# One matmul between two inner steps, a peak one chunk earlier, a store on another queue and an earlier flag load in a hash-attention and MLP kernel

## The chip, the cores and the metric

The kernel runs on one core of a Trainium2 chip. A core has five engines with queues of their own: TensorE (PE, with weight loads as PEld), VectorE (DVE), ScalarE (ACT), GpSimd (POOL) and SyncE (SP). SP, ScalarE and GpSimd issue DMA transfers. The metric is the device time of one execution in microseconds; lower is better.

## What is computed

```python
def _attn_ref(q, k, v, proj):                      # (4, 8, 768, 64) each, proj (64, 6)
    q_bucket, k_bucket = ...                       # 6 sign bits of q @ proj and k @ proj
    mask = q_bucket[:, :, :, None] == k_bucket[:, :, None, :]
    scores = np.where(mask, scale * np.matmul(q, k.transpose(0, 1, 3, 2)), -1e9)
    attn = softmax(scores)                         # sums have 1e-9 added
    return np.matmul(attn, v)

def _moe_ref(x, w_in, w_out):                      # x (3072, 512), d_ff 2048
    h = x @ w_in
    r = np.maximum(h, 0.0)
    return (r * r) @ w_out
```

The attention's output, its heads side by side, is the x of the second block.

## The kernel before

**Stages.** The first half of the span is the attention, pair of heads by pair of heads. Its softmax takes no maximum off; that is right as long as no score is large. So the second half also finds the largest sum of squares of any piece of q and k (a *peak*, 32 pieces of 128x768), and a flag says at the end whether a slow general path (`general`, line 1906) has to run instead. With the inputs here it does not run.

The second half is the two matrix products in three chunks of 1024 tokens (`i` = 0, 1, 2). Each chunk has a *hidden* stage (x times w_in, then relu squared, into the tiles b11 to b22) and a *project* stage (times w_out).

**Products by Strassen's scheme.** Each product is done with seven block products instead of eight (`product`, line 976, whose inner names one, two, three and five are copies of accumulators to SBUF by ScalarE at line 995). In the project stage there are seven outer products, k = 0 to 6, of seven inner ones each; an inner one (`add`, line 983) is four 128x256 matmuls at line 988. The order of the adds in `product` is fixed: acc[0] (copied to `one`), acc[1], acc[0] (copied to `two`), acc[2] (to `five`), acc[0] (to `three`), acc[2], acc[0].

**The hidden stage of chunks 1 and 2** runs `hidden_wide` (line 1329), twice for each n: half 0 and half 1. Of the seven outer factors, two are done whole: two 512-wide matmuls each at line 1313 (`add` in `outer_steps`, one per f in 0, 1) into the accumulator acc0. The others are split again: `inner_steps` (line 1226) gives four steps for each. In half 0 these are A and D. A step is one or two 256-wide matmuls at line 1245 into banks of PSUM, and a copy of a bank by ScalarE (lines 1255, 1261, 1264, 1271, 1279). The next step of the same factor adds into that same bank, so it waits until the copy has read it. For n = 0, half 0 has its own order, written out at lines 1341 to 1357; ScalarE copies the finished acc0 to the tile `tmp` (`two`, line 1324), which is used at line 1377.

**Peaks.** `mark` (line 1046) puts a peak into ScalarE's queue at the place where it stands (square with a sum, line 1039), and issues on GpSimd's queue the loads of the piece that the mark after the next will use (`load_peak`, line 1029, two buffers). The marks stand in the hidden stage's steps, in `rest` (called in the hook after acc[1]), `beside` (after `three`) and, where `then` has it, right after the copy to `two`. Chunk 1 has two in each k; chunk 2 has two in k = 0 and three in each k of 1, 2 and 3.

**Stores.** `put_out` (line 1598) turns a finished output block on VectorE and stores it in four pieces of 32 rows: those of the quarter (1, 1) on GpSimd's queue, all others on SP's. The last quarter of chunk 2 goes in parts (`put_part`, `put_last`): n = 0 on SP, n = 3 and n = 1 on SP and ScalarE in turn, n = 2 in two transfers at the very end. `in_turn` keeps their order of issue. The quarters come in the order n = 0, 3, 1, 2. From n = 3 on a scheduler places the instructions (`by_hand.close()`); before that they stand in the order of the code.

**Semaphores of transfers.** Each transfer issued by SP or ScalarE signals its end on one of eight semaphores, which are given out in turn over the whole program, and waits before its issue for the transfer that had the same one before. GpSimd's transfers have another eight of their own. At the end of the program SP waits for all sixteen and some others, in a fixed order: those of GpSimd first, then the eight of SP and ScalarE from the first to the last.

**The flag.** `values_load(slow)` (line 1007) makes each engine load the flag into a register; the branch at line 1933 reads it.

Of the kernel before, what the change touches and what calls it, by code (L numbers as in the profile page):

```python
# [34 lines left out]
def kernel(  # L35
# [10 lines left out]
    nc = tc.nc  # L46
# [9 lines left out]
    NFT = DM // P  # L56
# [10 lines left out]
    NCHUNK = B * S // NCH  # L67
# [704 lines left out]
    with by_hand:  # L772
# [532 lines left out]
        def outer_steps(i, n, half):  # L1305


            w, bt = w_unit.pop(i * NR + 2 * n + half), factors_x(i)
            acc = ps_m.tile([P, 512], FP32, name="acc0")

            def add(to, a, b, first, last):
                for f in range(NFT // 2):
                    nc.tensor.matmul(  # L1313
                        out=to, lhsT=w[:, PLACE[a], f], rhs=bt[b](f),
                        start=first and f == 0, stop=last and f == NFT // 2 - 1,
                        skip_group_check=True,
                    )

            def keep(of, name):
                if (name, half) == ("two", 0):  # L1320
                    t = p_y.tile([P, HN], FP32, name="tmp")
                else:
                    t = p_r.tile([P, 512], FP32, name=name, bufs=KEPT[name])
                nc.scalar.copy(out=t, in_=of)
                return t

            return w, acc, add, keep

        def hidden_wide(i, n, half):

            r0, r = n, NQ + n
            edge = (i, n) == (NCHUNK - 1, NQ - 1)
            w, acc, add, keep = outer_steps(i, n, half)
            own = own_factors(w, half)
            if half == 0:
                load_inner(i, n + 1)
                load_third_inner(i, n + 1, nc.sync)
                A = now["A"] = inner_steps(i, 0, w_inner[i, n][0], n > 0)
                D = now["D"] = inner_steps(i, 3, lambda a: own[a], n > 0)
                if n == 0:  # L1340
                    add(acc, 0, "11", True, False)
                    one = keep(acc, "one")
                    A[0]()
                    sums_inner(i, (3,))
                    mark()
                    add(acc, 4, "t2", False, True)
                    two = keep(acc, "two")
                    A[1]()
                    D[0]()
                    mark()  # L1350
                    A[2]()
                    D[1]()
                    A[3]()
                    D[2]()
                    sums_inner(i, (4,))
                    D[3]()
                    add_to(b11[:, r0], A[4][0], one)
                else:
                    A[0]()
                    D[0]()  # L1360
                    add(acc, 0, "11", True, False)
                    behind(0)
                    one = keep(acc, "one")
                    behind(1)
                    A[1]()
                    D[1]()
                    A[2]()
                    D[2]()
                    add_to(b11[:, r0], A[4][0], one)
                    behind(2)  # L1370
                    add(acc, 4, "t2", False, True)
                    two = keep(acc, "two")
                    A[3]()
                    behind(3)
                    D[3]()
                now["two"] = two
                add_in(D[4][0], two)
                gate_in(b11[:, r0])
                behind(4)
                sum_unit(i * NR + 2 * n + 1)  # L1380
                return
            A, D, two_0 = now["A"], now["D"], now["two"]
            B, C = inner_steps(i, 2, w_inner[i, n][2]), inner_steps(i, 1, w_inner[i, n][1])
            E = inner_steps(i, 4, lambda a: own[a])
            u0 = D[4]
            add(acc, 0, "11", True, False)
            one = keep(acc, "one")
            add_to(b11[:, r], A[4][1], one)
            B[0]()
            C[0]()  # L1390
            E[0]()
            gate_in(b11[:, r])
            behind(5)
            sum_unit(i * NR + 2 * n + 2)
            add(acc, 4, "t2", False, True)
            two = keep(acc, "two")
            add_in(u0[1], two)
            B[1]()
            C[1]()
            B[2]()  # L1400
            E[1]()
            C[2]()
            B[3]()
            E[2]()
            hB, hC, hE = B[4], C[4], E[4]

            def ahead(m):
                minus(b_t[:, m], b12[:, m], b11[:, m])

            def over(m):  # L1410
                minus(b12[:, m], b22[:, m], b12[:, m])

            put(hB[0], b12[:, r0], u0[0])
            C[3]()
            E[3]()
            if edge:
                ahead(r0)
                inner_sums(0, slice(n, n + 1))
                add_to(b22[:, r0], u0[0], hE[0])

                def hook():
                    add_to(b12[:, r], hB[1], u0[1])
                    gate_in(b12[:, r])
                    add_in(two, hE[1])
                    add_to(b21[:, r], hC[1], two)
                    add_to(b22[:, r], u0[1], hE[1])

                def with_two():
                    gate_in(b22[:, r0])
                    add_in(two_0, hE[0])  # L1430
                    add_to(b21[:, r0], hC[0], two_0)

                def with_five():
                    gate_in(b22[:, r])
                    over(r0)
                    over(r)

                def with_three():
                    gate_in(b21[:, r0])
                    gate_in(b21[:, r])  # L1440

                now["edge"] = dict(
                    hook=hook, early=lambda: ahead(r), two=with_two, five=with_five, three=with_three
                )
                return
            add_to(b22[:, r0], u0[0], hE[0])
            both = slice(n, NR, NQ)

            def sums_0():
                if i == 1:  # L1450
                    add_to(b12[:, r], hB[1], u0[1])
                else:
                    put(hB[1], b12[:, r], u0[1])
                add_to(b22[:, r], u0[1], hE[1])

            def gates_0():
                gate_in(b22[:, r0])

            def sums_1():
                add_in(two_0, hE[0])  # L1460
                add_to(b21[:, r0], hC[0], two_0)
                add_in(two, hE[1])

            def sums_2():
                add_to(b21[:, r], hC[1], two)

            def gates_1():
                if i == 1:
                    gate_in(b12[:, r])

            def gates_2():
                gate_in(b22[:, r])

            def gates_3():
                gate_in(b21[:, r0])

            def gates_4():
                gate_in(b21[:, r])

            steps = (  # L1480
                (sums_0, gates_0), (sums_1,),
                (sums_2, gates_1, lambda: ahead(both), gates_2, gates_3),
                (lambda: inner_sums(0, slice(n, n + 1)),), (gates_4,), (lambda: over(both),),
            )
            for m, some in enumerate(steps):
                behind_pair[m] = list(some)
# [111 lines left out]
        def put_out(i, ih, jh, n, o):  # L1598
# [4 lines left out]
            m0 = ih * HD + n * P  # L1603
            at = slice(i * NCH + jh * HN, i * NCH + (jh + 1) * HN)
            for a in range(P // 32):
                queue = nc.gpsimd if (ih, jh) == (1, 1) else nc.sync
                queue.dma_start(
                    out=out[at, m0 + a * 32:m0 + (a + 1) * 32].rearrange("(c i) j -> i c j", i=32),
                    in_=ot[a * 32:(a + 1) * 32].rearrange("i (c j) -> i c j", j=32),
                )  # L1610
# [11 lines left out]
        def put_part(n, o):  # L1622
# [6 lines left out]
            lo = (NCHUNK - 1) * NCH + col * QN  # L1629
            m0 = HD + row * P  # L1630
            for a in range(P // 32):
                in_turn(LATE[n][a].dma_start(
                    out=out[lo:lo + QN, m0 + a * 32:m0 + (a + 1) * 32].rearrange(
                        "(c i) j -> i c j", i=32
                    ),
                    in_=ot[a * 32:(a + 1) * 32].rearrange("i (c j) -> i c j", j=32),
                ))

        def put_last(n, o):

# [25 lines left out]
        def project(i):  # L1666
# [56 lines left out]
                close(1, 0, n)  # L1723

            more = i + 1 < NCHUNK
            uses = first_, seventh, fifth, third, second, sixth, fourth
            for k in range(7):
                b = OUTER[k][1]
# [40 lines left out]
                    minus(y21, y21, t2)  # L1769

                def rest():
                    if marks(i, k):
                        mark()
                    if (i, k) == (NCHUNK - 1, 4):
                        tops()
# [28 lines left out]
                        edge["early"]()  # L1804
                        turn_inner()

                then = {"two": mark} if i == NCHUNK - 1 and 0 < k < 4 else {}
                if edge:
                    then = dict(edge, five=lambda: (edge["five"](), rest()))
                product(  # L1810
# [301 lines left out]
```

## Time and profile before

| | |
|---|---|
| time, median of 3 runs | 847.46 us (847.46 to 849.12) |
| the profiled execution's own time | 848.54 us |
| its span, first to last instruction | 847.0 us |
| granted TensorE clock | 0.999 of full speed |
| instructions | 17534 |
| hidden stage of chunk 1, half 0 of n = 0 | from 494.8 us |
| project stage of chunk 1, k = 3 | from 620.3 us |
| hidden stage of chunk 2, half 0 of n = 0 | from 668.7 us |
| project stage of chunk 2, k = 0 | from 757.0 us |
| last transpose on TensorE | 843.1 us |

The profile is one execution. Its times are microseconds from the span's start; an engine's busy time leaves out register, branch, semaphore and DMA-issuing instructions, which the views by source line show as the engine's queue (SPq, ACTq, POOLq). A 32-bit matmul is recorded as two records: x4 of a 512-wide matmul are two matmuls. Ends of matmuls are modelled, so TensorE's pace is read from start to start.

### The profile page before, as it was taken

What the parts mean: (1) busy time and instruction counts of PE and PEld (TensorE: products, weight loads), DVE (VectorE), ACT (ScalarE), POOL (GpSimd) and SP (SyncE); (2) the same over time, 40 slices, a digit from 0 to 9 for tenths busy, and PEclk for the clock granted to TensorE, in tenths of its full rate; (3) what the DMA queues carried; (4) which work ended last, traced back from release to release, by engine and by line L of the source; (5) the groups of instructions that cost most, each with busy time, mean ns of one, the idle gap of its engine ahead of it and who ended that gap; (6) DMA issues with size and microseconds to landing.
All of it is one profiled execution on the core that took longest, in us unless ns stands there. A gap on an engine that the chain in (4) does not pass through costs nothing.

```text
span 847.0 us, 17534 instructions
## 1 busy us (share of the span) xinstructions
PE 841.0 (99%) x6710; PEld 558.3 (66%) x6710; DVE 748.7 (88%) x1081; ACT 461.3 (54%) x873; POOL 169.0 (20%) x285
## 2 busy tenths in 40 slices
PE   9999999999999999999999999999999999999998
PEld 4475444444444445544788877777888877778886
DVE  4898999999999988989899988868999877889787
ACT  5787787878777762222111148866322477765411
POOL 1321111303122200653121230002212400002202
PEclk9999999999999999999999999999999999999999
DMA  9966999978987626999977995418978964317767
GB/s 184 192 136 136 188 186 199 194 181 199 258 197 229 214 70 227 338 306 308 354 250 244 264 216 166 134 56 284 310 214 242 242 220 129 128 43 225 245 175 146
DMA packets 238296, 174.23 MB, mean 206 GB/s; under 512 B 166008, under 2 KB 196288, under 8 KB 238208
## 3 DMA queue, kind: packets, MB, share of 16 engines
q1 hardware_dynamic: 199792, 93.03, 44.5%
q0 software_dynamic: 16880, 43.92, 16.4%
q10 hardware_dynamic: 21536, 36.12, 13.9%
q8 instruction: 54, 0.88, 0.5%
q14 instruction: 34, 0.28, 0.1%
HBM read 129.64 MB, written 42.73 MB: 204 GB/s over the span
## 4 chain that ended last, share of the span: by engine, by line
PE 97%; ACT 1%; DVE 1%; DMA 1%; issue 0%; ACTq 0%; POOL 0%; POOLq 0%
PE acc L988 39%; PE st L478 18%; PE xo L532 15%; PE acc L1245 10%; PE acc L1313 7%; PE last L1245 4%; PE tot L589 1%; PE hash L396 1%; DMA raw_qk<-in_k_dram 1%; PE tp L342 0%; PE last L1313 0%; PE xo L371 0%; ACT b L1293 0%; DVE b L1303 0%; ACT raw_qk L1039 0%
## 5 line engine op out<-in xcount | busy, mean ns | idle before, releaser
L484 ACT ACTIVATE e<-st 128x768 f32<-128x768 f32 x192 | 155.5, 810 | 56.4 <-PE st L478 52.1
L532 PE MATMUL xo<-e,v_nat 64*64 64x385 f32 (+1 forms) x1520 | 156.9, 483 | 0.0
L988 PE MATMUL acc<-b,leaf 128*128 128x256 f32 x600 | 133.3, 379 | 0.4 <-ACT five L995 0.4
L988 PEld LDWEIGHTS acc<-b,leaf 128*128 128x128 f32 x600 | 113.8, 190 | 16.8 <-ACT five L995 0.8
L478 PE MATMUL st<-feat 64*64 64x384 f32 x1056 | 108.1, 482 | 0.0
L444 POOL DMA_DIRECT2D bits<-signed x120 | 62.2, 521 | 206.5 <-ACT signed L433 204.7
L532 PEld LDWEIGHTS xo<-e,v_nat 64*64 64x64 f32 (+1 forms) x1520 | 58.9, 133 | 65.3 <-issue 54.5
L988 PE MATMUL acc<-t,leaf 128*128 128x256 f32 x336 | 76.0, 379 | 0.0
L988 PEld LDWEIGHTS acc<-t,leaf 128*128 128x128 f32 x336 | 63.8, 190 | 8.8 <-issue 0.2
L478 PE MATMUL st<-bits 64*64 64x384 bf16 x768 | 66.2, 324 | 0.1
L520 DVE TENSOR_TENSOR total<-total,e 128x1536 f32<-128x1536 f32 x32 | 56.0, 1749 | 7.6 <-ACT e L484 6.8
L1034 POOL DMA_DIRECT2D raw_qk<-in_q_dram x32 | 17.3, 541 | 213.3 <-ACT raw_qk L1039 111.0
L520 DVE TENSOR_TENSOR t_x<-t_x,e 128x1536 f32<-128x1536 f32 x32 | 55.8, 1744 | 3.8 <-ACT e L484 3.7
L988 PE MATMUL acc<-x,w_unit 128*128 128x512 f32 (+1 forms) x144 | 56.5, 545 | 0.0
L478 PEld LDWEIGHTS st<-feat 64*64 64x64 f32 x1056 | 38.4, 133 | 27.3 <-issue 24.2
L988 PE MATMUL acc<-b_t,leaf 128*128 128x256 f32 x240 | 53.8, 379 | 0.0
L995 ACT COPY two<-acc 128x256 f32<-128x256 f32 (+1 forms) x29 | 12.5, 431 | 73.9 <-PE acc L988 53.3
L995 ACT COPY one<-acc 128x256 f32<-128x256 f32 (+1 forms) x29 | 12.5, 431 | 71.2 <-PE acc L988 47.8
L478 PE MATMUL st<-t_x 64*64 64x384 f32 x480 | 50.2, 482 | 0.0
L988 PEld LDWEIGHTS acc<-b_t,leaf 128*128 128x128 f32 x240 | 45.6, 190 | 6.2
L478 PEld LDWEIGHTS <-bits 64*64 64x64 bf16 x768 | 24.7, 107 | 34.7 <-issue 33.5
L988 PEld LDWEIGHTS acc<-x,w_unit 128*128 128x128 f32 x144 | 27.3, 190 | 26.6 <-issue 25.2
(248 smaller groups left out, 1570.9 us busy)
## 6 DMA issues: line engine op xcount, KB each, us to landing
leaf<-w_out ACTq DMA_DIRECT2D x132, 256.0 KB, 3.5
raw<-in_moe_w_in_dram SPq DMA_DIRECT2D x8, 1024.0 KB, 6.5
raw<-in_moe_w_out_dram SPq DMA_DIRECT2D x8, 1024.0 KB, 7.6
w_unit<-w_in SPq DMA_DIRECT2D x8, 896.0 KB, 8.5
w_out<-sums POOLq DMA_DIRECT2D x16, 448.0 KB, 8.7
v_nat<-in_v_dram SPq DMA_DIRECT2D x16, 384.0 KB, 5.1
x_all<-x_raw SPq DMA_DIRECT2D x16, 384.0 KB, 3.2
raw_qk<-in_q_dram POOLq DMA_DIRECT2D x32, 192.0 KB, 3.9
```

What stands on the lines that cost most here:

```text
L396: nc.tensor.matmul(out=banks[g * NR_B:(g + 1) * NR_B, h, 0:HS], lhsT=projs[rows, h * D:h * D + NR_B], rhs=feat[pr][rows, w, c * HS:(c + 1) ...
L444: nc.gpsimd.dma_start(out=t[h * D:h * D + NBITS + 1, w, c * HS:(c + 1) * HS], in_=signed[pr % 2][at:at + NBITS + 1, h],)
L478: nc.tensor.matmul(out=st[k * HK:(k + 1) * HK, h, 0:HS], lhsT=src[1][rows, key], rhs=src[0][rows, cut], start=first, stop=not first, skip_ ...
L484: nc.scalar.activation(out=key_of(pr, kt)[:, :, i, 0:HS], in_=st[:, :, 0:HS], func=ACTF.Exp, scale=scale)
L520: nc.vector.tensor_tensor(out=totals[pr], in0=totals[pr], in1=e, op=ALU.add)
L532: return nc.tensor.matmul(out=outs[pr][h * D:(h + 1) * D, c, 0:HS + 1], lhsT=nat[pr, "v_nat"][rows, h, kt * D:(kt + 1) * D], rhs=key_of(pr ...
L589: done = nc.tensor.matmul(out=to[g * 32:(g + 1) * 32, c2], lhsT=ones[rows], rhs=totals[pr][rows, h, c, c2 * QS:(c2 + 1) * QS], start=whole ...
L988: nc.tensor.matmul(out=acc[to][:, at_c], lhsT=a(i), rhs=b(i)[:, at_c], start=first and i == 0, stop=last and i == n - 1, skip_group_check= ...
L995: nc.scalar.copy(out=t, in_=acc[of])
L1034: nc.gpsimd.dma_start(out=raw_qk[i][:, w], in_=flat[:, i * n:(i + 1) * n])
L1245: nc.tensor.matmul(out=banks[to], lhsT=w(a), rhs=b, start=start, stop=stop, skip_group_check=True)
L1313: nc.tensor.matmul(out=to, lhsT=w[:, PLACE[a], f], rhs=bt[b](f), start=first and f == 0, stop=last and f == NFT // 2 - 1, skip_group_check ...
```

## The change

There are four edits. (1) In `hidden_wide`, n = 0, half 0, of the two matmuls at line 1313 that add the factor 4 into acc0 the second (and with it the copy to `two`) comes after the inner step D[2] instead of right behind the first. This happens in chunk 1 and in chunk 2. (2) One mark fewer in `rest` of chunk 2, k = 1, and one more after `two` of chunk 1, k = 3; the number of peaks stays 32. (3) The last of the four pieces of the very first output block (chunk 0) is stored from GpSimd's queue. (4) SP's load of the flag stands ahead of the first store of n = 3, held there by a dependency that sets the order and waits for nothing.

```diff
@@ outer_steps
-            def add(to, a, b, first, last):
-                for f in range(NFT // 2):
+            def add(to, a, b, first, last, parts=range(NFT // 2)):
+                for f in parts:
@@ hidden_wide
                     sums_inner(i, (3,))
                     mark()
-                    add(acc, 4, "t2", False, True)
-                    two = keep(acc, "two")
+                    add(acc, 4, "t2", False, False, (0,))
                     A[1]()
                     D[0]()
...
                     D[2]()
                     sums_inner(i, (4,))
+                    add(acc, 4, "t2", False, True, (1,))
+                    two = keep(acc, "two")
                     D[3]()
@@ put_out
-                queue = nc.gpsimd if (ih, jh) == (1, 1) else nc.sync
+                queue = nc.gpsimd if (ih, jh) == (1, 1) or (i, ih, jh, n, a) == (0, 0, 0, 0, 3) else nc.sync
@@ put_part
-                in_turn(LATE[n][a].dma_start(
+                store = LATE[n][a].dma_start(
...
+                if (n, a) == (3, 0):
+                    flag_load = [
+                        x for x in nc.cur_bb.bb.instructions
+                        if x.engine == store.ins.engine and "TensorLoad" in type(x).__name__
+                    ][-1]
+                    tc.add_manual_dep(store.ins, flag_load.name, ISSUE)
+                in_turn(store)
@@ project
+            WITH_TWO = {(1, 3)} | {(NCHUNK - 1, k) for k in (1, 2, 3)}
...
-                    if marks(i, k):
+                    if marks(i, k) and (i, k) != (NCHUNK - 1, 1):
                         mark()
...
-                then = {"two": mark} if i == NCHUNK - 1 and 0 < k < 4 else {}
+                then = {"two": mark} if (i, k) in WITH_TWO else {}
```

More of the change, by code (lines that the diff above doesn't have):

```diff
@@ L1636, in put_part @@
                     in_=ot[a * 32:(a + 1) * 32].rearrange("i (c j) -> i c j", j=32),
-                ))
+                )
+                if (n, a) == (3, 0):
[5 more added lines that the diff above has]
+                in_turn(store)
         def put_last(n, o):
```

## The prediction

> **What bounds the kernel now.** I read the page first: busy times and the chain of waits.
>
> ```profile
> PE 841.0 (99%) x6710; PEld 558.3 (66%) x6710; DVE 748.7 (88%) x1081; ACT 461.3 (54%) x873; POOL 169.0 (20%) x285
> PE 97%; ACT 1%; DVE 1%; DMA 1%; issue 0%; ACTq 0%; POOL 0%; POOLq 0%
> ```
>
> TensorE sets the end nearly everywhere, and the change takes no matmul away. So only two things can move the time: gaps between matmuls, and the tail behind the last one. I looked for the gaps in the timeline of TensorE (start and duration in us, engine, line, operation, tiles; in brackets the idle time and what ended it), start to start. A 256-wide matmul counts as two records 0.216 us apart (a run of sixteen takes 3.45 us, below), a 512-wide one as two records 0.43 apart; what is more is lost. In the stages that the change touches three places lose more than 0.1 us. The first two are alike, the last inner step D[3] in chunk 1 and in chunk 2:
>
> ```profile
> 503.45 0.59 PE L1245 MATMUL last<-t_x,w_unit 128*128 128x256 f32 x2
> 504.08 0.70 PE L1245 MATMUL acc<-o,w_unit 128*128 128x256 f32 x2
> 504.62 0.59 PE L1313 MATMUL acc<-x,w_unit 128*128 128x512 f32 x1
> ...
> 677.35 0.59 PE L1245 MATMUL last<-t_x,w_unit 128*128 128x256 f32 x2
> 677.98 0.70 PE L1245 MATMUL acc<-o,w_unit 128*128 128x256 f32 x2
> 678.51 1.02 PE L1313 MATMUL acc<-x,w_unit 128*128 128x512 f32 x2
> ...
> 677.55 0.37 ACT L1271 COPY other<-acc 128x256 f32<-128x256 f32 x1
> ```
>
> The pair at 503.45 should be followed at 503.88; the next starts at 504.08, 0.20 late, and then takes 0.54 us to the matmul behind it instead of 0.43: 0.11 more. At 677.35 it is the same, and the reader sees why: D[3] goes into the bank that the copy at line 1271 empties, and this copy ends at 677.92. Both places lose 0.31 us.
>
> The third place is the second of the seven products of chunk 2 (k = 1):
>
> ```profile
> 772.52 3.62 PE L988 MATMUL acc<-t,leaf 128*128 128x256 f32 x16
> 775.97 1.89 PE L988 MATMUL acc<-b,leaf 128*128 128x256 f32 x8
> 778.30 3.72 PE L988 MATMUL acc<-b,leaf 128*128 128x256 f32 x16 [0.44 <-ACT five L995]
> ...
> 774.44 0.37 ACT L995 COPY two<-acc 128x256 f32<-128x256 f32 x1 [2.08 <-PE acc L988]
> 777.05 0.84 ACT L1039 ACTIVATE raw_qk<-raw_qk 128x768 f32<-128x768 f32 x1 [2.23 <-DMA raw_qk<-in_k_dram]
> 777.89 0.35 ACT L995 COPY five<-acc 128x256 f32<-128x256 f32 x1
> ...
> 771.04 5.91 DMA raw_qk<-in_k_dram
> ```
>
> Eight records from 775.97 end their turn at 777.70; the next starts at 778.30, 0.60 late, and its run is 0.10 longer than a free one (3.72 against 3.62): 0.70 us. The releaser is the copy to "five". It stood in ScalarE's queue behind a peak (the square of a piece of q and k), and the peak waited until 776.95 for its load, issued at 771.04 and 5.91 us on its way.
>
> **The change part by part.** *One of two L1313 matmuls, chunks 1 and 2, moved behind D[2].* It removes nothing; 0.86 us of TensorE work leaves the place between A[0] and A[1] and goes in front of D[3]. There it covers the gap: D[2] then ends 0.86 us earlier, the copy at 1271 too, and D[3] finds its bank empty 0.7 us before its turn. Gain 0.31 twice. What loses its cover is A[1], which writes the bank that A[0]'s copy reads:
>
> ```profile
> 671.24 1.96 PE L1313 MATMUL acc<-t_x,w_unit 128*128 128x512 f32 x4
> 673.03 0.59 PE L1245 MATMUL acc<-t,sum 128*128 128x256 f32 x2
> ...
> 671.06 0.38 ACT L1255 COPY h<-acc 128x256 f32<-128x256 f32 x1
> 673.24 0.59 ACT L1324 COPY tmp<-acc 128x512 f32<-128x512 f32 x1 [0.59 <-PE acc L1313]
> ```
>
> A[1] comes 0.86 earlier, at 672.17; that copy ends at 671.44. So 0.7 us of cover stays, and nothing waits. On ScalarE the 0.59 us copy of the whole accumulator moves behind the inner steps as well, so the copies that A[2], D[1] and A[3] need come forward with their matmuls and keep their distance. Bounds: if all of that cover failed, A[1] would lose at most 0.31 as D[3] does now; a gain beyond the gap itself is out. I take no loss, as the nearest row shows the copy long done. Behind D[3], the second half loses another 0.04 in each chunk, since VectorE and ScalarE arrive late from it:
>
> ```profile
> 682.82 1.92 PE L1313 MATMUL acc<-t_x,w_unit 128*128 128x512 f32 x4
> ```
>
> (1.92 where 1.88 is free.) VectorE's chain comes forward with the copy, so this goes too. Together 2 x (0.31 + 0.04) = 0.70 us.
>
> *One peak moved from k = 1 of chunk 2 to k = 3 of chunk 1.* The count of peaks stays. In chunk 2 the first of the three peaks of k = 1 goes, so the peak behind "two" uses the load that this first one had used, issued at 767.51:
>
> ```profile
> 767.51 0.54 POOL L1034 DMA_DIRECT2D raw_qk<-in_k_dram  x1
> ...
> raw_qk<-in_k_dram POOLq DMA_DIRECT2D x1, 192.0 KB, 2.7
> ```
>
> That is in place at 770.2, over 4 us before "two" ends (774.81). "five" is then bound by TensorE alone, and 0.70 us goes. The load that came late now feeds the third peak, which stands behind "three", due after 778: it lands at 776.95, and behind that peak only the "one" of the next product waits, five microseconds later. In chunk 1 the added peak stands between "two" and "five" of k = 3; POOL issues one more pair of loads ahead of the eight stores of that chunk's sixth product, in time it had idle.
>
> ```profile
> 625.69 0.37 ACT L995 COPY two<-acc 128x256 f32<-128x256 f32 x1 [2.06 <-PE acc L988]
> 627.42 0.37 ACT L995 COPY five<-acc 128x256 f32<-128x256 f32 x1 [1.35 <-PE acc L988]
> ...
> L1034 POOL DMA_DIRECT2D raw_qk<-in_k_dram x1: 537/537/537, 619.1 to 619.1; - x1
> DMA to landing us min/median/max: 3.5/3.5/3.6
> ```
>
> ScalarE idles 1.35 us there, and a peak with its read-out takes 1.0. The load for it (the view by tile: durations in ns, first and last start; below it the time from issue to landing, in us) is the one issued at 619.1, here by 622.7, 3.4 us before it is wanted. Cost nothing; the bound above is in the rivals.
>
> The Trainium skill's page "SBUF — State Buffer", section "SBUF: two separate sides", says that VectorE in its two-port modes starves the descriptor writing of GpSimd's queue, so such loads seem to hang for as long as VectorE is busy. The row of those stretches (busy time of TensorE, weight loads, VectorE, ScalarE, POOL):
>
> ```profile
> 764.00:776.00 12.00, 12.00 (x58) 10.55 (x57) 11.86 (x15) 8.06 (x18) 3.19 (x6) 1.00 0.76 233
> ```
>
> VectorE was busy for 11.86 of 12 us, and of the two loads issued there one took 2.7 and the other 5.9. By the rule both would be slow, and a load at 5.9 would still be in place at 773.4, before "two"; the sum stays, and only rival C below gets its chance from it.
>
> *One store of chunk 0 goes from SP's queue to POOL's.* POOL had nothing to do at that time; SP issued eight stores, so one fewer frees it sooner for the loads behind:
>
> ```profile
> 473.05 6.95 SPq L1607 DMA_DIRECT2D out_dram<-h  x8
> ...
> 486.03 2.61 POOL L1607 DMA_DIRECT2D out_dram<-h  x4 [15.41 <-DVE h L1602]
> ```
>
> POOL's issue costs 0.65 (2.61 / 4) inside 15 us of idleness. Queued behind it are the first two peak loads, wanted only in the hidden stage near 497. No time either way. Its effect is elsewhere: transfers from SP and ScalarE take eight completion semaphores in turn. With one fewer, every later one sits one place earlier in that round. The built programs list SP's closing waits in a fixed order, and ScalarE's last store is the fifth of twelve before and the twelfth after.
>
> *SP's load of the flag goes ahead of the stores of n = 3.* The tail now:
>
> ```profile
> 843.85 0.36 ACTq L1652 DMA_DIRECT2D out_dram<-h  x1
> out_dram<-h ACTq DMA_DIRECT2D x1, 64.0 KB, 1.8
> ...
> L1007 POOLq TENSOR_LOAD <-slow x1: 822/822/822, 837.8 to 837.8; - x1
> L1007 SPq TENSOR_LOAD <-slow x1: 523/523/523, 844.2 to 844.2; - x1
> L1933 SPq COMPARE_BRANCH  x1: 50/50/50, 844.8 to 844.8; - x1
> L2108 SPq EVENT_SEMAPHORE  x4: 28/28/28, 845.3 to 845.5; - x4
> L2108 SPq EVENT_SEMAPHORE  x8: 27/28/28, 845.6 to 846.0; - x8
> ...
> 840.94 0.32 SPq L1632 DMA_DIRECT2D out_dram<-h  x1
> ...
> 841.79 0.45 DVE L1628 STREAM_TRANSPOSE h<-o 128x256 f32<-128x256 f32 x1
> ```
>
> The last store lands at 843.85 + 1.8 = 845.6. SP passes four waits, stands at the fifth until that landing, then walks eight in 0.4 us, and everything else waits for it. With the flag loaded earlier (0.52 us, from about 840.4, where SP has issued the stores of n = 0 and waits for the one at 840.94; if it takes the 0.82 of POOL's load, that store is 0.3 late, and SP's next but one waits for a transpose until 842.24 anyway) the walk begins 0.6 earlier, at 844.7; eleven waits at 0.06 are past by 845.4, and the twelfth passes at the landing. The end comes 0.4 earlier. Either edit alone gives 0.1 or less, since the landing or the eight waits stay. Bounds: 0 (landing later) and 0.6 (the load and its gap). I take 0.42, seven waits of 0.06.
>
> The Trainium skill's page "DMA: Bandwidth & Descriptors", section "Anatomy of one DMA — SWDGE (gpsimd) path", gives such a transfer about 2.0 us fixed plus its bytes. An estimate by it: 843.85 + 2.15 = 846.0 for the landing, a tail gain of 0.05, and a sum of 1.45 instead of 1.82. The trace's 1.8 decides.
>
> Sum: 0.70 + 0.70 + 0.42 = 1.82 us. Against the profiled execution, 848.54 (847.0 of span and 1.5 around it), that is 846.72; against the median of the runs shown, 847.46, it is 845.64. These four executions spread over 1.66 us and their middle is 848.0, which would give 846.2. I set 845.9, between the two.
>
> **The rivals.** *A: the tail stays.* If the landing is late, or the wait list does not bind, 1.40 remains: about 846.1 from the median. For it: only one trace shows where the fifth wait stood. Against: four waits, a gap, then eight.
>
> *B: the gain of the inner steps is absorbed later.* VectorE is 99% busy at 764 to 776; if it, not TensorE, sets the pace into k = 1 of chunk 2, the 0.70 from the inner steps is given back: 1.12, 846.3. Against it: no gap is put down to VectorE there, and its chain starts from the same earlier matmuls.
>
> *C: slower, the late peak load moves to k = 3 of chunk 1.* The longest such load took
>
> ```profile
> DMA to landing us min/median/max: 10.7/10.8/10.9
> ```
>
> With that, the peak begins at 630.0, "five" at 630.9, and the matmul 0.41 behind (777.89 to 778.30), at 631.3 against a turn of 628.95: 2.35 lost and 0.1 of a longer run. It decides from a landing of 8.5 us on, eats the whole gain at 10.2, and at 10.9 gives 847.46 + 0.63 = 848.1. For it: POOL issues behind ScalarE's peaks, as now at k = 1. Against: the long one was issued beside the load of the next x, which has no copy at 619, where 3.5 was measured.
>
> *D: the change doesn't do what it says.* The instruction orders show the moved matmul, peak, store and flag load, so only the cover can fail: A[1] loses what D[3] gains, 0.70 + 0.42 = 1.12, again 846.3.
>
> **How the numbers follow.** Forecast 0.62, A 0.15, B and D together 0.12, C 0.07, a cost not seen 0.04. A measurement of this kernel tells 0.2% (1.7 us) from no change. The forecast's 1.82 lies just beyond that line and the runs spread by as much, so it counts two thirds for faster (0.41) and one third for the same (0.21); A, B and D give 0.06 for faster and 0.21 for the same. C lies 0.08% above the median, so most of it is the same as well (0.05 of 0.07); the rest, and 0.04 for a cost that I don't see, is slower by over 0.2%. Faster 0.47, same 0.47, slower 0.06. The range goes from 844.8 (845.64 less half the spread) to 848.0, close to C.
>
> **What would show it.** Right: D[3] 0.43 behind the pair before it in both chunks; the peak behind "two" at k = 1 without a wait for its load, and the run of sixteen at its turn; no such wait at k = 3 of chunk 1; SP's twelve closing waits starting about 0.6 after its last store's issue ends, the last one at the landing. The span falls from 847.0 to about 845.2. Wrong: a new gap before A[1] or A[2], a peak load of over 8.5 us at k = 3, a landing later than the walk by more than a wait, or gaps of VectorE's in k = 1 and 2 of chunk 2 that weren't there.

## The result and the profile after

| | before | after |
|---|---|---|
| median of 21 runs each, taken side by side | 847.65 us (846.85 to 849.74) | 846.46 us (845.45 to 847.39) |
| ratio, 95% interval | | 0.9982 (0.9976 to 0.9988) |
| the profiled execution's own time, its span | 848.54, 847.0 us | 845.68, 844.1 us |
| hidden stage of chunk 1 begins | 494.76 us | 493.83 us |
| from there to the last matmul ("the stretch") | 348.48 us | 347.03 us |
| from the issue of ScalarE's last store to the span's end ("the tail") | 3.14 us | 2.67 us |

The changed kernel is faster by 0.18% (0.12 to 0.24%). Times the 847.65 of before that is 1.5 us, with an interval of 1.0 to 2.0. The two profiled executions differ by more, 2.86 us: 0.93 up to 493.83, where the programs are alike but for one store, 1.45 in the stretch and 0.47 in the tail. The first of the three belongs to the executions: it is whole by 54 us, where a run of sixteen matmuls at line 532 starts at 54.70 in before and at 53.77 in the changed kernel, far ahead of every edited line. Of the 1.45, 0.68 is the moved matmul, 0.70 the gap at k = 1 and 0.07 a loss at 599.8 of before that no edit touches.

Busy times and the chain of waits on the page of the changed kernel:

```profile
PE 839.1 (99%) x6710; PEld 554.3 (66%) x6710; DVE 748.5 (89%) x1081; ACT 461.4 (55%) x873; POOL 169.9 (20%) x286
PE 99%; ACT 0%; issue 0%; DVE 0%; POOL 0%; POOLq 0%
```

The 1% each that ScalarE, VectorE and transfers had of the chain before is gone. That alone shows no gain: e12 below, the kernel before in another execution, has the same second line.

The inner steps of chunk 2, in the timeline of the changed kernel (start, duration, engine, line, operation):

```profile
669.04 1.03 PE L1245 MATMUL acc<-x,sum 128*128 128x256 f32 x4
669.90 1.10 PE L1313 MATMUL acc<-t_x,w_unit 128*128 128x512 f32 x2
670.84 0.59 PE L1245 MATMUL acc<-t,sum 128*128 128x256 f32 x2
671.27 0.59 PE L1245 MATMUL last<-t,sum 128*128 128x256 f32 x2
...
675.15 0.59 PE L1245 MATMUL last<-t_x,w_unit 128*128 128x256 f32 x2
675.59 1.02 PE L1313 MATMUL acc<-t_x,w_unit 128*128 128x512 f32 x2
676.44 0.59 PE L1245 MATMUL acc<-o,w_unit 128*128 128x256 f32 x2
676.88 1.88 PE L1313 MATMUL acc<-x,w_unit 128*128 128x512 f32 x4
```

The moved matmul stands at 675.59, D[3] comes at 676.44, 0.86 behind it, and lasts 0.59: nothing is lost. A[1], at 670.84, is 0.86 behind the matmul that stayed, plus 0.08 that this one loses itself (1.10 where 1.02 is free); it comes right behind the end of ScalarE's copy to "one" (669.83), and lost the same 0.08 before (1.96 for the two, where 1.88 is free). So A[1] pays nothing.

The product k = 1 of chunk 2, in the same timeline:

```profile
767.28 0.54 POOL L1034 DMA_DIRECT2D raw_qk<-in_k_dram  x1 [1.44 <-issue]
770.84 3.62 PE L988 MATMUL acc<-t,leaf 128*128 128x256 f32 x16
772.77 0.37 ACT L995 COPY two<-acc 128x256 f32<-128x256 f32 x1 [3.08 <-PE acc L988]
773.03 0.85 ACT L1039 ACTIVATE raw_qk<-raw_qk 128x768 f32<-128x768 f32 x1
774.29 4.91 PE L988 MATMUL acc<-b,leaf 128*128 128x256 f32 x22
774.49 0.37 ACT L995 COPY five<-acc 128x256 f32<-128x256 f32 x1 [0.52 <-PE acc L988]
```

The peak behind "two" starts when "two" ends, without a wait for its load: the load issued at 767.28 took 3.3 us and was in place at 770.6, 2.4 us before. (The 1.44 us of idle time ahead of its issue come up again with e9, e11 and e12.) "five" now waits for TensorE and no longer the other way round, and the records run through. At k = 3 of chunk 1 the added peak does the same:

```profile
624.35 0.37 ACT L995 COPY two<-acc 128x256 f32<-128x256 f32 x1 [2.06 <-PE acc L988]
624.62 0.85 ACT L1039 ACTIVATE raw_qk<-raw_qk 128x768 f32<-128x768 f32 x1
626.08 0.37 ACT L995 COPY five<-acc 128x256 f32<-128x256 f32 x1 [0.52 <-PE acc L988]
```

The view by tile gives the load for that peak, and for all loads of its stretch the us from issue to landing:

```profile
L1034 POOL DMA_DIRECT2D raw_qk<-in_k_dram x1: 539/539/539, 618.0 to 618.0; - x1
DMA to landing us min/median/max: 3.6/3.7/3.8
```

In place by 621.8 at the latest, at least 2.8 us before it is wanted.

The tail, from the timeline and the views by source line (durations in ns, then first and last start in us):

```profile
841.38 0.35 SPq L1660 DMA_DIRECT2D out_dram<-h  x1
841.47 0.36 ACTq L1660 DMA_DIRECT2D out_dram<-h  x1
...
L1007 SPq TENSOR_LOAD <-slow x1: 492/492/492, 838.1 to 838.1; - x1
L1942 SPq COMPARE_BRANCH  x1: 50/50/50, 841.8 to 841.8; - x1
L2117 SPq EVENT_SEMAPHORE  x12: 28/28/28, 842.3 to 843.2; - x12
...
DMA to landing us min/median/max: 1.6/1.6/1.7
```

SP reads the flag at 838.1, where it read it at 844.2 before. Its twelve closing waits begin 0.56 us after its last store's issue ends (841.73) and the last passes at 843.2, where ScalarE's store lands (841.47 + 1.7). The tail fell from 3.14 to 2.67. From the landing to the span's end it fell by 0.42 (1.39 to 0.97); the rest is a store that landed 1.70 us after its issue instead of 1.76.

### The profile page after: what moved, and what is told of

The parts are those of the page before. It is cut to its first block, busy times and chain, and to the rows that moved or that the text cites. A ratio compares the mean times of both kernels' runs of the same rounds, so it can differ in the third digit from the quotient of the medians.

```text
span 844.1 us, 17531 instructions
## 1 busy us (share of the span) xinstructions
PE 839.1 (99%) x6710; PEld 554.3 (66%) x6710; DVE 748.5 (89%) x1081; ACT 461.4 (55%) x873; POOL 169.9 (20%) x286
## 4 chain that ended last, share of the span: by engine, by line
PE 99%; ACT 0%; issue 0%; DVE 0%; POOL 0%; POOLq 0%
PE acc L988 41%; PE st L478 18%; PE xo L532 15%; PE acc L1245 10%; PE acc L1313 7%; PE last L1245 4%; PE tot L589 1%; PE hash L396 1%; PE last L1313 0%; PE tp L342 0%; PE xo L371 0%; PE hash L406 0%; PE xo L406 0%; ACT e L484 0%; PE acc L1655 0%
## 5 line engine op out<-in xcount | busy, mean ns | idle before, releaser
L532 PEld LDWEIGHTS xo<-e,v_nat 64*64 64x64 f32 (+1 forms) x1520 | 56.9, 133 | 67.3 <-issue 54.7
```

The source lines that it names most:

```text
L532: return nc.tensor.matmul(out=outs[pr][h * D:(h + 1) * D, c, 0:HS + 1], lhsT=nat[pr, "v_nat"][rows, h, kt * D:(kt + 1) * D], rhs=key_of(pr ...
```

## The experiments

Timed kernels were compared with runs of before on the same chip. The stretch and the tail are read from each profile as in the table above.

| kernel | ratio to before (95%) | hidden stage from | stretch | tail |
|---|---|---|---|---|
| e1, edit 1 alone | 0.9990 (0.9981 to 0.9999) | 496.14 | 347.03 | 3.15 |
| e2, edit 2 alone | 0.9999 (0.9989 to 1.0008) | 494.57 | 347.73 | 3.15 |
| e3, edit 3 alone | one run | 494.80 | 347.73 | 3.07 |
| e4, edit 4 alone | one run | 495.37 | 347.96 | 3.12 |
| e5, edits 3 and 4 | one run | 494.74 | 349.01 | 2.69 |
| e6, both matmuls moved | one run | 494.68 | 347.58 | 2.67 |
| e7, added peak at k = 0 | one run | 493.58 | 349.07 | 2.75 |
| e8, another order | 0.9982 (0.9971 to 0.9992) | 493.90 | 347.07 | 2.69 |
| e9, without edit 2 | 0.9988 (0.9979 to 0.9997) | 494.24 | 347.67 | 2.68 |
| e10, a second order | 0.9984 (0.9975 to 0.9993) | 494.24 | 347.41 | 2.69 |
| e11, before again | one run | 495.82 | 348.56 | 3.15 |
| e12, before a third time | one run | 494.57 | 347.89 | 3.14 |

**e1: the moved matmul alone**, with the new argument of `add` in `outer_steps` as in the change.

```diff
@@ before, hidden_wide, n = 0, half 0
-                    add(acc, 4, "t2", False, True)
-                    two = keep(acc, "two")
+                    add(acc, 4, "t2", False, False, (0,))
                     A[1]()
...
+                    add(acc, 4, "t2", False, True, (1,))
+                    two = keep(acc, "two")
                     D[3]()
```

> The kernel before with the moved matmul alone. My theory: in chunk 1 and chunk 2 the gaps before and behind D[3] (0.31 us) and the 0.04 in half 1 go, A[1] and A[2] lose nothing; 0.70 us in all, so the span from the first matmul of the hidden stage of chunk 1 (494.8 before) to the last matmul shrinks by 0.70 and the 0.60 + 0.10 before 778.30 stays. Rival B: VectorE takes the 0.70 back by k = 1 of chunk 2, and that same stretch shrinks by less than 0.3. Rival for the 0.93 us that the changed kernel gained in the first 47 us of its profile, where nothing was changed: if the change made it, this run's start differs from before's in one way for all kernels with the edit; if it is the execution, the starts of this call's four profiles scatter by up to about 1 us whatever the edit.

D[3] is on time in both chunks, the 0.04 behind it is gone, and the tail is that of before. The ratio says 0.8 us (0.1 to 1.6) by 848.13, the median of before beside it. What was not foreseen is at k = 1 of chunk 2, where the marks are those of before:

```profile
775.07 0.37 ACT L995 COPY two<-acc 128x256 f32<-128x256 f32 x1 [2.08 <-PE acc L988]
776.58 0.84 ACT L1039 ACTIVATE raw_qk<-raw_qk 128x768 f32<-128x768 f32 x1 [1.13 <-DMA raw_qk<-in_k_dram]
776.60 3.62 PE L988 MATMUL acc<-b,leaf 128*128 128x256 f32 x16
777.42 0.35 ACT L995 COPY five<-acc 128x256 f32<-128x256 f32 x1
```

The peak still waits for its load, but the load took 4.80 us instead of 5.91, "five" is done in time, and the run of sixteen is whole. The 0.70 us gap of before is not there.

**e2: the moved peak alone.**

```diff
@@ before, project
+            WITH_TWO = {(1, 3)} | {(NCHUNK - 1, k) for k in (1, 2, 3)}
...
-                    if marks(i, k):
+                    if marks(i, k) and (i, k) != (NCHUNK - 1, 1):
                         mark()
...
-                then = {"two": mark} if i == NCHUNK - 1 and 0 < k < 4 else {}
+                then = {"two": mark} if (i, k) in WITH_TWO else {}
```

> The kernel before with the moved peak alone. My theory: the 0.70 us before the matmul at 778.30 goes, the peak behind two of k = 1 of chunk 2 waits for no load, the added peak at k = 3 of chunk 1 costs TensorE nothing; the stretch from the hidden stage of chunk 1 to the last matmul shrinks by 0.70, and the gaps of 0.31 before D[3] stay. Rival C: a gap appears in k = 3 of chunk 1, up to 2.4 us, if its load takes over 8.5 us.

No gap at k = 1 and none at k = 3 of chunk 1; D[3] is late by 0.30 as before. The stretch is 0.70 over that of e1, which is just the price of edit 1. The ratio shows no gain; its interval reaches from 0.9 us less to 0.7 us more.

**e3 and e4: the store alone, the flag load alone.**

```diff
@@ e3: before, put_out
-                queue = nc.gpsimd if (ih, jh) == (1, 1) else nc.sync
+                queue = nc.gpsimd if (ih, jh) == (1, 1) or (i, ih, jh, n, a) == (0, 0, 0, 0, 3) else nc.sync
@@ e4: before, put_part
-                in_turn(LATE[n][a].dma_start(
+                store = LATE[n][a].dma_start(
...
+                if (n, a) == (3, 0):
+                    flag_load = [
...
+                    tc.add_manual_dep(store.ins, flag_load.name, ISSUE)
+                in_turn(store)
```

> The kernel before with the one store on GpSimd's queue alone. My theory: nothing before the tail moves (stretch from the hidden stage of chunk 1 to the last matmul as before within 0.1); ScalarE's last store is the last of SP's twelve waits, but SP starts them 0.6 later than the changed kernel, so from the issue of that store to the end of the span it takes about 3.0 us (3.1 before, 2.6 in the changed kernel). Rival: the place of the wait is what counts alone, and the tail is 2.65 here.

> The kernel before with the earlier flag load alone. My theory: SP starts its twelve waits 0.6 earlier, but stands at the fifth until the last store lands and then walks seven more; the tail from the issue of ScalarE's last store to the end stays at 3.0 to 3.1 us. Rival: the flag load alone makes the tail, and it is 2.65 here.

The tails are 3.07 and 3.12. Why neither is enough is seen in SP's closing waits. With the store alone:

```profile
843.13 0.36 ACTq L1652 DMA_DIRECT2D out_dram<-h  x1
...
L2108 SPq EVENT_SEMAPHORE  x12: 27/28/28, 844.5 to 845.2; - x12
```

With the flag load alone:

```profile
843.94 0.36 ACTq L1659 DMA_DIRECT2D out_dram<-h  x1
...
L2115 SPq EVENT_SEMAPHORE  x4: 28/28/28, 844.8 to 845.0; - x4
...
L2115 SPq EVENT_SEMAPHORE  x8: 27/28/28, 845.7 to 846.1; - x8
```

In e3 nothing blocks the twelve, but they begin 1.4 us behind the store's issue, since the flag load still stands between, and take their 0.7 us. In e4 they begin 0.8 behind it, stop at the fifth until the store lands at about 845.7, and eight are left to walk. In both, the gap at k = 1 of chunk 2 is absent, with the marks of before.

**e5: edits 3 and 4 together**, the two diffs above on before.

> Before with the store of the first block on POOL's queue and with SP's earlier load of the flag, and nothing else. Theory (the tail needs both edits): from the issue of ScalarE's last store to the span's end 2.65 to 2.7 us, as the changed kernel has, against 3.14 before and 3.07 and 3.12 with either edit alone; SP's twelve closing waits begin about 0.6 us earlier and the last one ends at the landing. Rival (the tail's gain comes from elsewhere, as from other times of the stores after the earlier edits): 3.0 or more. The late D[3] stays in both chunks. The 0.70 us gap in the second product of chunk 2 (k = 1), whose marks are those of before here, should be absent as in the three kernels with these marks that were run, if it was one execution's late load; if it is there, it is a frequent event.

```profile
844.35 0.36 ACTq L1659 DMA_DIRECT2D out_dram<-h  x1
...
L2115 SPq EVENT_SEMAPHORE  x12: 28/28/28, 845.2 to 846.1; - x12
```

Tail 2.69: only the two together give it, and the earlier edits have no part in it. At k = 1 of chunk 2 the gap is back (timeline, and at the end the load's row in the chain of waits with issue and time to landing):

```profile
776.51 1.89 PE L988 MATMUL acc<-b,leaf 128*128 128x256 f32 x8
777.55 0.84 ACT L1039 ACTIVATE raw_qk<-raw_qk 128x768 f32<-128x768 f32 x1 [2.19 <-DMA raw_qk<-in_k_dram]
778.39 0.35 ACT L995 COPY five<-acc 128x256 f32<-128x256 f32 x1
778.80 1.56 PE L988 MATMUL acc<-b,leaf 128*128 128x256 f32 x6 [0.40 <-ACT five L995]
...
773.03 0.54 POOL L1034 DMA_DIRECT2D raw_qk<-in_k_dram  x1 [1.44 <-issue]
773.03 4.41 DMA raw_qk<-in_k_dram
```

Eight records from 776.51 end their turn at 778.24; the next comes at 778.80, 0.56 late, and a longer run behind it makes 0.67. Here the load was not slow but issued late, at 773.03. So the expectation that the gap would be absent was wrong.

**e6: both matmuls behind D[2].**

```diff
@@ after, hidden_wide, n = 0, half 0
-                    add(acc, 4, "t2", False, False, (0,))
                     A[1]()
...
-                    add(acc, 4, "t2", False, True, (1,))
+                    add(acc, 4, "t2", False, True)
                     two = keep(acc, "two")
```

> The changed kernel with both of the matmuls at line 1313 behind D[2], so that A[1] follows A[0] with no 512-wide matmul between. Theory (a step waits for the copy of the bank that the step before it in the same factor has filled, some 0.9 us from its start, so one matmul of 0.86 us is just enough cover): A[1] has its turn some 0.1 us before that copy ends and comes 0.2 to 0.3 us late, with a longer run behind it, once per chunk; D[3] has twice the cover it needs and is on time. Rival (the cover of A[1] was never needed, half 0 is bound by something else): no gap before A[1], and the span is that of the changed kernel or less by the 0.08 us that the first matmul of the pair now waits for ScalarE.

```profile
670.16 1.03 PE L1245 MATMUL acc<-x,sum 128*128 128x256 f32 x4
671.27 0.70 PE L1245 MATMUL acc<-t,sum 128*128 128x256 f32 x2
671.80 0.59 PE L1245 MATMUL last<-t,sum 128*128 128x256 f32 x2
...
670.84 0.38 ACT L1255 COPY h<-acc 128x256 f32<-128x256 f32 x1
```

A[1]'s turn is 671.02 (670.16 + 0.86). It starts at 671.27, just behind the end of the copy at 1255 (671.22): 0.25 late, and 0.10 more in its run. Twice 0.35 lost and twice 0.08 won at the first matmul make 347.58, as measured. So the cover of A[1] was needed, and one matmul is enough of it.

**e7: the added peak at k = 0 of chunk 1.**

```diff
@@ after, project
-            WITH_TWO = {(1, 3)} | {(NCHUNK - 1, k) for k in (1, 2, 3)}
+            WITH_TWO = {(1, 0)} | {(NCHUNK - 1, k) for k in (1, 2, 3)}
```

> The changed kernel with the added peak of chunk 1 behind the copy to two of the product k = 0 instead of k = 3, where in the profile of before one of these loads took 10.9 us beside the copy of the next x. Theory (a peak whose load is late holds ScalarE's queue, and through the copy behind it TensorE): the peaks at k = 0 or 1 of chunk 1 wait for their load if it takes more than 8 us, and TensorE has a gap of 0.5 to 1.5 us with a releaser on ScalarE (a copy to one or five) between 592 and 605 us. Rival (a late load costs nothing since the copy behind the peak is not what TensorE waits for): loads of 8 us or more with no gap. If the loads come within 5 us, the run tells nothing of the mechanism, and shows again that the time to landing is not fixed by the place.

```profile
597.30 0.84 ACT L1039 ACTIVATE raw_qk<-raw_qk 128x768 f32<-128x768 f32 x1 [5.63 <-DMA raw_qk<-in_k_dram]
598.50 0.36 ACTq L1580 DMA_DIRECT2D leaf<-w_out  x1
599.33 3.72 PE L988 MATMUL acc<-t,leaf 128*128 128x256 f32 x16 [1.16 <-ACT one L995]
605.15 2.18 PE L988 MATMUL acc<-b,leaf 128*128 128x256 f32 x9 [0.38 <-DMA leaf<-w_out]
...
598.50 6.51 DMA leaf<-w_out
```

The load took 10.6 us, the peak held ScalarE for 5.63, and TensorE lost 1.43 at 599.33 (1.32 of start and 0.10 of a longer run). Rival C's mechanism is real, at another place than where the change puts the peak. What the expectation missed is the second loss, 0.61 at 605.15: the loads of leaves that stood behind the peak in ScalarE's queue went out late too. The one issued here at 598.50 went out at 595.01 in the changed kernel, and took about as long there (6.18 us). The two make the 2.04 by which the stretch exceeds that of the changed kernel.

**e8 and e10: two other orders of half 0.**

```diff
@@ after, hidden_wide, n = 0, half 0 (as in e10)
                     mark()
+                    D[0]()
                     add(acc, 4, "t2", False, False, (0,))
                     A[1]()
-                    D[0]()
+                    D[1]()
                     mark()
                     A[2]()
-                    D[1]()
-                    A[3]()
                     D[2]()
                     sums_inner(i, (4,))
                     add(acc, 4, "t2", False, True, (1,))
                     two = keep(acc, "two")
+                    A[3]()
                     D[3]()
```

In e8 A[3] stands directly behind D[2].

> The changed kernel with another order in half 0 of n = 0: A[0], D[0], the first of the two matmuls at line 1313, A[1], D[1], A[2], D[2], A[3], the second one, D[3]. Theory (only the distance to the step before in the same factor counts): all steps have at least 0.86 us of other work between them, the first of the matmuls has ScalarE's copy to one behind it by then, so the 0.08 us that it waits in each chunk go and no gap comes: 0.15 us less than the changed kernel in the profile, which the timing cannot tell from it (ratio to before 0.998). Rival (the order also sets when VectorE and ScalarE get their sums and copies, and the later first matmul delays half 1 or the next n): gaps of 0.1 us or more in the stretch behind, and a ratio of 0.999 or more.

> The changed kernel with half 0 of n = 0 in the order A[0], D[0], first matmul at line 1313, A[1], D[1], A[2], D[2], second matmul, A[3], D[3]. In the order tried before this one a loss of 0.10 us came at A[3], one step behind D[2], where ScalarE's copy of A[2]'s bank stood behind a peak. Theory (the distance to the copy decides, with what stands ahead of that copy on ScalarE): with D[2] and the matmul between A[2] and A[3] both losses are gone, the 0.08 us at the first matmul and the 0.10 us at A[3]; the stretch from the first hidden matmul of chunk 1 to the last matmul is 346.85 to 346.9 us against 347.03 of the changed kernel. The timing cannot tell 0.15 us: ratio 0.998. Rival (the loss belongs to the peak's new place and goes to another step): a loss of 0.1 us elsewhere in the half, stretch 347.0 or more.

In e8 the 0.08 at the first matmul went, and 0.10 came at A[3]:

```profile
500.40 0.85 ACT L1039 ACTIVATE raw_qk<-raw_qk 128x768 f32<-128x768 f32 x1
501.24 0.36 ACT L1271 COPY h<-acc 128x256 f32<-128x256 f32 x1
...
501.66 0.69 PE L1245 MATMUL acc<-t,sum 128*128 128x256 f32 x2
```

The copy stands behind a peak and ends at 501.60, just ahead of A[3], which starts in its turn but runs 0.10 longer. In e10 both losses are gone. Its stretch is 347.41 all the same, since 0.52 was lost at 597 to 599, in the products k = 0 and 1 of chunk 1, which the edit does not touch; without it, 346.89 as expected. Both are faster than before by the same 0.17% or so as the changed kernel, and cannot be told from it.

**e9, e11, e12: how often the gap at k = 1 comes.** e9 is the changed kernel with the three lines of edit 2 as they were before; e11 and e12 are the kernel before without an edit.

> The changed kernel without the moved peak: the marks are those of before, the other three edits stay. Theory now (the peak behind the copy to two at k = 1 of chunk 2 waits for its load in every execution with these marks; TensorE waits only when the load lands later than about 5.2 us behind the issue of 771, which was so in two of the five executions seen): the peak shows a wait for its load; a gap of 0.5 to 0.8 us is there or not; the ratio to before lies between that of the changed kernel and 0.3 us above it: 0.998 to 0.999. Rival (the 0.70 us gap is there as a rule, and the executions without it were the exceptions): gap there, ratio 0.999 or more. Stretch from the first hidden matmul of chunk 1 to the last matmul 347.03 us without the gap, 347.7 with it; tail 2.65 to 2.7.

> The kernel before, unchanged, to see in one more execution whether TensorE's gap of 0.7 us at k = 1 of chunk 2 is there. Theory (the gap is a matter of one execution's load): without it or with it, and the peak behind the copy to two waits for its load either way; with the gap only if that load lands after 5.2 us or is issued later. Rival (it is a fixed cost of these marks): 0.6 to 0.75 us.

> The kernel before once more, for the same count: the gap at k = 1 of chunk 2 there or not, the wait of the peak for its load there in both cases. D[3] late by 0.30 us in both chunks and the tail 3.1 us, as constants of this kernel.

The eight executions with the old marks, the load that the peak behind "two" waits for, and what TensorE lost. "Late by" is its landing (issue plus time) less the start of the matmuls between which the gap opens (775.97 in before):

| | issue, us | to landing, us | late by, us | lost, us |
|---|---|---|---|---|
| before | 771.04 | 5.91 | 0.98 | 0.70 |
| e5 | 773.03 | 4.41 | 0.94 | 0.67 |
| e9 | 771.63 | 3.99 | 0.50 | 0.24 |
| e3 | 772.46 | 3.76 | 0.28 | 0 |
| e4 | 771.84 | 4.91 | -0.02 | 0 |
| e1 | 771.68 | 4.80 | -0.13 | 0 |
| e12 | 770.97 | 4.71 | -0.22 | 0 |
| e11 | 772.89 | 4.54 | -0.39 | 0 |

The peak waited for its load in all eight; TensorE paid in three, and what it paid beyond the 0.10 of a longer run grows one for one with the lateness from 0.37 on. The mean is 0.20 us. In the six executions with the moved peak (after, e2, e6, e7, e8, e10) nothing was lost there.

The eight are of two kinds. With edit 3, the store on GpSimd's queue (e5, e9, e3), GpSimd issues the second load of this pair 1.98 us behind the first; 1.44 of that it stands idle for nothing that the profile shows ("issue"). Without edit 3 it is 0.53. So this load goes out 3.48 us ahead of the matmuls where the gap opens instead of 4.93, and TensorE pays once it takes more than 3.9 us instead of 5.3. Of the three with edit 3 two paid, 0.30 us in the mean; of the five without it one, 0.14 in the mean. All eight kernels with edit 3 have the 1.98 there, the changed one too, where the moved peak leaves the 2.4 us of cover seen above. Why one more store on that queue does it stays open. The ratio of e9, 0.9988 against 0.9982 of the changed kernel, fits a small loss without edit 2, but the intervals overlap.

## Why the prediction came out as it did

The median, 846.46, lies 0.56 above the 845.9 foreseen and inside the range; the gain of 0.18% lies just short of the line of 0.2% that the prediction named, where the 1.82 us lay just beyond it.

| term | predicted | measured |
|---|---|---|
| moved matmul | 0.70 | 0.70: e1's stretch against e2's and e3's; by the gaps, 2 x (0.30 + 0.04) |
| moved peak | 0.70 | 0.14 in the mean of the five executions without edit 3, 0.70 in the one profiled |
| store and flag load | 0.42, either alone 0.1 or less | 0.45 to 0.47 (after, e5), alone 0.07 and 0.02 |
| sum | 1.82 | 1.30 |

*The moved matmul* was right in mechanism and size. It is half of what the change is worth, and e1's ratio bears it out. e6 shows from the other side that the cover that was left for A[1] is what A[1] needs.

*The moved peak* is the step that was mis-sized. The working took the 0.70 us of one execution's trace for a price that every execution pays. The chain was read rightly: load, peak, "five", TensorE. But the row at its head, a load of 5.91 us, was one draw: in the four other executions that issue it at the same place (e1, e4, e11, e12) it took 4.5 to 4.9, and TensorE pays from 5.3 on. The mean of 0.14 rests on five executions, one of which paid; the timing of e2 can neither show nor exclude it. The other half of this step held: the peak at k = 3 costs nothing.

*The store on GpSimd's queue* was taken to cost no time either way. In the changed kernel it costs none, but it holds a load of k = 1 of chunk 2 back by 1.44 us, which the prediction did not see. With the old marks that leaves the load 3.9 us instead of 5.3 before TensorE pays, so edit 2 covers what edit 3 brings, and the two are not independent. Two of three executions paid against one of five; so few do not settle how much it costs.

*The tail* was right, and for the reason given, down to the last wait at the landing. The rival estimate rested on the Trainium skill's page "DMA: Bandwidth & Descriptors", section "Anatomy of one DMA — SWDGE (gpsimd) path", which gives about 2.0 us fixed plus the bytes for transfers of GpSimd's queue. The store here is one of ScalarE's, so the section does not speak of it. By the estimate the gain would have been 0.05; the landing took 1.7 here, and the runs side with the trace.

*The rivals.* A fell with the tail of 2.67. B fell: in e1 and after no gap of VectorE's stands in k = 1 or 2 of chunk 2, and e1's stretch is 0.70 shorter than e3's. C did not happen at k = 3, where the load took 3.8 at most; e7 shows the mechanism at k = 0, and with it a second loss, by the leaves behind, that the working had left out. D fell with the row of A[1].

The measured terms add up to 1.30, inside the 1.0 to 2.0 of the ratio. Set against the 847.65 of before they give 846.35, 0.11 from the median. The prediction's own sum gave 845.64, 0.82 below the median: 0.52 of that are the terms, 0.19 the time of before (847.65 in 21 runs, 847.46 in the three shown), and 0.11 stays open. The step from 845.64 to 845.9 was made for the scatter of the executions and not for the gap; that it made the miss smaller is partly luck.

## What to carry to other kernels

A gap that ends at a transfer can be a draw and not a constant. Before its whole length is counted as a gain, look at how much cover the transfer has, and in how many executions it would be short. D[3]'s gap, which hangs on copies and matmuls alone, came out alike in all seven profiles that have it. Look also at what else an edit moves in the queue that it goes into: the store on GpSimd's queue held back a load there 280 us later. Where two steps in the same bank follow each other, spread the independent work so that each has just enough; and where a closing walk of waits and a landing both bind, moving one alone shows next to nothing.

## What the runs showed of the hardware

- Three executions of the same program, before, e11 and e12, had spans of 847.0, 848.1 and 846.2 us. Their hidden stages began at 494.76, 495.82 and 494.57, so over half of the scatter is in place before any edited matmul. (e11 also lost 0.85 us at 665, behind a copy to "two" that came late, which no other execution shows.) The changed kernel's 0.93 us ahead of the stretch is of that size, and is counted as no part of its gain.
- Time to landing had two faces. At k = 0 of chunk 1 the second of the two loads of one pair took 10.6 to 11.0 us in every execution; at k = 1 of chunk 2 it took 3.8 to 5.9. VectorE's share does not sort the latter. Busy time of TensorE, weight loads, VectorE, ScalarE and POOL between 770 and 777 us, first in before, where the load took 5.91, then in e12, where it took 4.71:

```profile
770.00:777.00 7.00, 7.00 (x34) 6.17 (x33) 6.97 (x9) 2.15 (x7) 2.13 (x4) 1.00 0.89 295
```

```profile
770.00:777.00 7.00, 7.00 (x35) 6.15 (x34) 6.96 (x9) 3.29 (x10) 2.14 (x4) 1.00 0.87 298
```

  VectorE was busy for 6.97 and 6.96 of 7 us. The Trainium skill's page "SBUF — State Buffer", section "SBUF: two separate sides", has VectorE in its two-port modes hold back the loads of GpSimd's queue; whether its work here is of that kind no row shows. But ScalarE's queue was slow as well: its two loads of leaves issued at 771.0 and 771.5 in before took 6.1 and 6.2 us, those at 770.9 and 771.4 in e12 4.7 and 4.8. So what made the difference was not on GpSimd's queue alone; what it was stays open.
- A loss of 0.2 to 0.6 us at 597 to 600 came in some executions (e4, e5, e9, e10, e12) and not in others with the same code there. In e5 the weight loads waited for a late leaf and then for the peak behind a 10.7 us load. No run moved only that place's loads, so whether the loss can be had stays open.
